# Linear attention and gated feed-forward: high weight words converted in PSUM, integer additions on GpSimd, k and v loaded as 112 and 3 rows, a new order

## The chip, the cores and the metric

The kernel runs on one core of a Trainium2 chip. The metric is the device time of one execution in microseconds. The kernel before was run three times: 1007.83, 1008.34 and 1012.99 us, median 1008.34. One execution was also profiled.

## The reference

Eight batches, eight heads, 576 tokens, head dimension 64; then a gated feed-forward network with 4608 tokens, model width 512 and inner width 1536.

```python
q_s = exp(q - max(q, -1)); q_s /= sum(q_s, -1) + 1e-9          # over the head dimension
k_s = exp(k - max(k, 2));  k_s /= sum(k_s, 2) + 1e-9           # over the tokens
kv  = einsum('bhsd,bhse->bhde', k_s, v)
x   = einsum('bhsd,bhde->bhse', q_s, kv)  ->  (4608, 512)
xn  = x / sqrt(mean(x * x, -1) + 1e-6) * rms_g
g   = xn @ w_gate
out = (g * sigmoid(g) * (xn @ w_val)) @ w_out
```

The three weight matrices arrive as float64, so each number is two 32-bit words, and the kernel makes float32 of them itself.

## The kernel before, in words

**Stages.** The 4608 tokens are cut into 9 blocks of 512. In each block the inner width is cut into 12 tiles of 128, so the feed-forward part has 108 steps, numbered `s` = 0 to 107. For one step, `f1` multiplies the block's x with a gate tile and a value tile (into two `ps_gv` banks of PSUM), `g_mul`, `silu` and `h_mul` combine them, and `f2` multiplies the result with a tile of the output weights and adds it up in four `ps_o` banks. Attention for the heads runs in pairs `g` = 0 to 3, per batch for k and v (`k_load`, `k_max`, `k_tr`, `k_top`, `k_diag`, `k_rows`, `k_sub`, `k_exp`, `k_mm`) and per block for q (`q_...`), and is spread between the feed-forward steps of the blocks before. Its PSUM tiles come from two `ps_a` banks, those of batch 0 from the `ps_o` banks, which are not yet in use then.

**Split products.** TensorE multiplies in a faster, shorter float32 format (float32r). A number is split into a high part (`w_hi`, `o_hi`, `h_hi`, a cast) and a low part (`w_lo`, `o_lo`, `h_lo`, number minus high part), and three products are added: `f1` is 24 matmuls in all, `f2` 12. For tiles 0 to 8 there is no `h_hi`, `h_lo`, `o_hi`, `o_lo`, and `f2` multiplies in plain float32, with four matmuls that the trace shows as two records each. Line 855 chooses the form. Copies and casts are recorded at line 329, products with a scalar at 334 (ScalarE) and 336 (VectorE).

**Weight conversion.** For tile `i` (0 to 11) and matrix `a` (gate, value, out), `load_w` (line 359) brings 512 columns of two-word numbers into a raw buffer. There are four raw buffers, two of which lie in the place of the later tiles' finished weights (line 319). `conv_low` (370, ScalarE) scales the low words to the three bits that belong to the fraction. `conv_mul` (374, ScalarE) scales the high words as floats, straight into the finished tile `W`. `conv_shift` (377) shifts that tile in place by three bits and clears the sign, `conv_sign` (382) puts the sign back from the raw word, both on VectorE. `conv_add` (387) adds the low bits as integers, on VectorE (letter D) or GpSimd (letter P, and without a letter). Gate and value are converted together (1024 columns) from tile 1 on, the output weights alone (512).

**Order.** All steps are written out in one string, `ORDER`, and issued in that order; each engine runs its own instructions strictly in it. A name is a step, its numbers are its arguments, and a letter says the engine: A ScalarE, D VectorE, P GpSimd. All DMAs are issued by SyncE, also in that order, so a load that waits for its buffer holds the loads behind it. `warm.n` are matmuls without use that keep TensorE busy.

**k and v loads.** From batch 1 on, 576 tokens lie as 115 rows of 5 tokens and one row with the last token. `k_load` (line 415) issues one DMA for the 115 rows of both heads (422) and one for the last row (423). `v_load` (438) issues one for the 115 rows of each head (446) and one for the last row (449). Batch 0 lies as 96 rows of 6.

Of the kernel before, what the change touches and what calls it, by code (L numbers as in the profile page):

```python
# [27 lines left out]
k_diag.0.1:A load_w.0.2 k_mm.0.0 q_exp.0.1 k_load.1.0 k_max0.0.2 k_rows.0.1 warm.2.2 q_eps0.0.0 k_max0.0.3 load_w.2.0
k_tr.0.2 warm.2.6 load_w.2.1 warm.2.10 load_w.1.2 q_rec0.0.0 k_top.0.2 k_tr.0.3 load_w.3.0 q_mul0.0.0:D k_diag.0.2:A
load_w.3.1 k_rows.0.2 k_sub.0.1 q_sub0.0.2:P warm.2.11 q_load0.1.0 q_max0.0.3 q_t0.0.0 k_exp.0.1 q_sum0.0.1  # L30
q_sub0.0.3:P q_exp.0.2 load_w.2.2 k_top.0.3 warm.2.3 q_c0.0.0:A k_sub.0.2 k_load.1.1 k_diag.0.3:A k_mm.0.1 q_exp.0.3
k_eps.0.0 q_eps0.0.1 load_w.3.2 k_rec.0.0 k_exp.0.2 q_rec0.0.1 q_sum0.0.2 k_rows.0.3 q_mul0.0.1:P warm.2.7
# [5 lines left out]
v_load.1.0 q_c0.0.3:A x_lo.0.1 q_x0.0.2 conv_mul.0.2.1:A conv_sign.0.1.1 n_sum0.1 conv_add.0.0.1:D conv_mul.1.0.2:A
x_hi.0.2:D conv_add.0.1.1:P q_x0.0.3 x_sq.0.2 k_max.1.0 conv_mul.2.0.2:A n_sum0.2 x_lo.0.2 x_sq.0.3 warm.2.8 warm.2.13
x_hi.0.3:A w_hi.0.0.2:D n_sum0.3 conv_low.2.0.2 conv_shift.1.0.2 x_lo.0.3 w_lo.0.0:P f1.0.0.0.0 f1.0.1.0.0  # L40
conv_mul.1.2.1:A f1.0.0.0.1 n_t.0 f1.0.0.0.2 conv_low.1.2.1 f1.0.0.0.3 f1.0.1.0.1 w_lo.0.1:D f1.0.1.0.2 f1.0.1.0.3
f1.0.0.1.0 n_y0.0 f1.0.0.1.1 conv_low.3.0.2 f1.0.0.1.2 conv_sign.1.0.2 f1.0.0.1.3 f1.0.1.1.0 f1.0.1.1.1 f1.0.1.1.2
f1.0.1.1.3 n_y1.0 conv_mul.3.0.2:A f1.0.0.2.0 conv_add.1.0.2:P f1.0.0.2.1 f1.0.0.2.2 f1.0.0.2.3 f1.0.1.2.0 f1.0.1.2.1
f1.0.1.2.2 conv_mul.2.2.1:A f1.0.1.2.3 q_max0.1.0 k_tr.1.0 conv_low.2.2.1 n_rows.0 q_sub0.1.0:P w_hi.1.0.2:A k_top.1.0
g_mul.0 v_ones.1.1 k_diag.1.0:A v_load.1.1 q_exp.1.0 w_lo.1.0:D k_rows.1.0 f1.1.0 silu.0 conv_shift.0.2.1 w_lo.1.1:D
conv_sign.0.2.1 conv_shift.2.0.2 conv_mul.3.2.1:A h_mul.0 conv_add.0.2.1:P conv_low.3.2.1 k_sub.1.0 f1.1.1 load_w.4.0
conv_sign.2.0.2 k_exp.1.0 load_w.4.1 load_w.4.2 q_sum0.1.0 conv_add.2.0.2:D f2.0 q_eps0.1.0 w_hi.2.0.2:D q_rec0.1.0
# [5 lines left out]
conv_low.5.0.2 load_w.6.1 w_lo.3.1:D load_w.6.2 f1.3.0 conv_shift.4.0.2 conv_mul.5.0.2:A q_max0.1.1 kv_lo.1.0:P
conv_low.5.2.1 conv_sign.4.0.2 conv_mul.5.2.1:A q_sub0.1.1:D f1.3.1 conv_add.4.0.2:D q_exp.1.1 g_mul.3 w_hi.4.0.2:D
silu.3 f2.2 q_sum0.1.1 w_lo.4.0:D conv_shift.3.2.1 conv_low.6.0.2 q_eps0.1.1 conv_sign.3.2.1 q_rec0.1.1 conv_low.6.2.1
h_mul.3 conv_add.3.2.1:P conv_mul.6.0.2:A k_max.1.2 k_tr.1.1 f1.4.0 q_mul0.1.1:P load_w.7.0 conv_mul.6.2.1:A
load_w.7.1 k_top.1.1 q_max0.1.2 k_diag.1.1:A load_w.7.2 q_load.2.0 w_lo.4.1:D conv_shift.5.0.2 k_rows.1.1 f1.4.1
# [5 lines left out]
conv_low.8.0.2 conv_sign.5.2.1 h_mul.5 w_lo.6.1:P conv_low.8.2.1 n_cols.0 v_ones.1.3 conv_add.5.2.1:D v_load.1.3
conv_shift.7.0.2 f1.6.0 q_eps0.1.2 conv_sign.7.0.2 q_rec0.1.2 conv_add.7.0.2:D f1.6.1 q_mul0.1.2:D w_hi.7.0.2:A
load_w.10.0 g_mul.6 load_w.10.1 load_w.10.2 w_lo.7.0:D silu.6 q_load.2.1 conv_shift.6.2.1 w_lo.7.1:D k_tr.1.2 f2.5
conv_sign.6.2.1 k_top.1.2 h_mul.6 conv_add.6.2.1:P k_diag.1.2:A k_max.1.3 conv_mul.8.0.2:A conv_shift.7.2.1 q_max0.1.3
conv_mul.8.2.1:A k_rows.1.2 q_t0.1.2 conv_shift.8.0.2 conv_low.10.0.2 f1.7.0 k_sub.1.2 q_sub0.1.3:P q_c0.1.2:A
# [859 lines left out]
```

## Time and profile before

| | |
|---|---|
| runs, us | 1007.83, 1008.34, 1012.99 |
| profiled execution, us | 1011.01 |
| its span, first to last instruction, us | 1009.2 |
| mean granted TensorE clock | 0.998 |
| TensorE busy | 992.5 us, 98% of the span, 4884 matmul records |
| VectorE busy | 514.4 us, 51% |
| ScalarE busy | 595.5 us, 59% |
| GpSimd busy | 683.5 us, 68% |
| read from and written to memory | 47.25 MB and 9.44 MB |

In the profile PE is TensorE, PEld its weight loads, DVE VectorE, ACT ScalarE, POOL GpSimd, SP SyncE (SPq its queue of DMA issues). `L826` is line 826 of the kernel. Times count from the first instruction. A line such as `ps_gv<-xh,wh` says what is written and what is read. Busy time is time in which at least one instruction of the engine runs, so the times of single instructions, which overlap a little, add up to slightly more.

### The profile page before, as it was taken

The numbers are of one execution on the slowest core, as the hardware profiler recorded it, in microseconds if no ns is written. First come the engines' busy times: TensorE is split into PE (matmuls) and PEld (weight loads), VectorE is DVE, ScalarE is ACT, GpSimd is POOL, SyncE is SP. The second block draws the span as 40 slices with busy tenths as digits, with TensorE's granted clock in tenths as the row PEclk, the third lists the DMA queues.
The fourth block names the chain that finished last, engine by engine and source line by source line (L and its number), as shares of the span: only waits on it lengthen the run. The fifth ranks groups of instructions, "written<-read, shape, count | busy, mean of one in ns | idle before, by whom it ended". The sixth has DMA issues, their size and how long they took to land.

```text
span 1009.2 us, 14153 instructions
## 1 busy us (share of the span) xinstructions
PE 992.5 (98%) x4884; PEld 795.7 (79%) x4884; DVE 514.4 (51%) x1191; ACT 595.5 (59%) x832; POOL 683.5 (68%) x601
## 2 busy tenths in 40 slices
...
DMA packets 128507, 57.60 MB, mean 57 GB/s; under 512 B 100620, under 2 KB 122420, under 8 KB 128436
## 3 DMA queue, kind: packets, MB, share of 16 engines
...
HBM read 47.25 MB, written 9.44 MB: 56 GB/s over the span
## 4 chain that ended last, share of the span: by engine, by line
PE 92%; SPq 4%; DMA 4%; ACT 0%; issue 0%; DVE 0%; ACTq 0%
PE ps_gv L826 57%; PE ps_o L865 29%; PE ps_a L704 2%; PE ps_a L505 2%; DMA w<-in_moe_w_out_dram 1%; SPq L365 1%; DMA w<-in_moe_w_val_dram 1%; SPq L446 1%; DMA raw<-in_moe_w_out_dram 1%; PE ps_a L487 1%; SPq L449 1%; DMA w<-in_k_dram 1%; SPq L443 0%; PE ps_a L754 0%; PE ps_a L633 0%; SPq L587 0%
## 5 line engine op out<-in xcount | busy, mean ns | idle before, releaser
L803 POOL TENSOR_TENSOR wl<-w,wh 128x512 fp32r<-128x512 f32 x203 | 262.2, 1300 | 107.3 <-ACT wh L329 81.3
L826 PE MATMUL ps_gv<-xh,wh 128*128 128x512 f32 x864 | 240.4, 400 | 0.9 <-ACT wh L329 0.7
L826 PE MATMUL ps_gv<-xl,wh 128*128 128x512 f32 x864 | 232.4, 391 | 0.0
L826 PE MATMUL ps_gv<-xh,wl 128*128 128x512 f32 x864 | 232.1, 391 | 0.0
L826 PEld LDWEIGHTS ps_gv<-xl,wh 128*128 128x128 f32 x864 | 162.8, 188 | 35.2
L826 PEld LDWEIGHTS ps_gv<-xh,wl 128*128 128x128 f32 x864 | 162.8, 188 | 35.0
L826 PEld LDWEIGHTS ps_gv<-xh,wh 128*128 128x128 f32 x864 | 157.1, 188 | 36.2 <-issue 1.9
L831 DVE TENSOR_TENSOR gs<-ps_gv,r 128x512 f32<-128x512 f32 x108 | 74.5, 690 | 214.9 <-PE ps_gv L826 189.1
L835 ACT ACTIVATE gs<-gs 128x512 f32<-128x512 f32 x108 | 68.3, 633 | 162.8 <-DVE gs L831 162.3
L847 POOL TENSOR_TENSOR hl<-gs,hh 128x512 fp32r<-128x512 f32 x99 | 129.0, 1303 | 14.9 <-ACT hh L329 14.4
L838 DVE TENSOR_TENSOR gs<-ps_gv,gs 128x512 f32<-128x512 f32 x108 | 74.2, 687 | 122.2 <-PE ps_gv L826 117.1
L811 POOL TENSOR_TENSOR ol<-w,oh 128x512 fp32r<-128x512 f32 x99 | 128.8, 1302 | 9.5 <-ACT oh L329 7.6
L329 ACT CAST wh<-w 128x1024 fp32r<-128x1024 f32 x92 | 96.6, 1050 | 40.6 <-PE ps_gv L826 31.9
L865 PE MATMUL ps_o<-oh,hh 128*128 128x512 f32 x396 | 108.8, 395 | 0.0
L865 PE MATMUL ps_o<-ol,hh 128*128 128x512 f32 x396 | 106.6, 390 | 0.0
L865 PE MATMUL ps_o<-oh,hl 128*128 128x512 f32 x396 | 106.6, 390 | 0.0
L329 ACT CAST oh<-w 128x512 fp32r<-128x512 f32 x99 | 61.3, 619 | 74.5 <-PE ps_o L865 73.9
L865 PEld LDWEIGHTS ps_o<-ol,hh 128*128 128x128 f32 x396 | 74.3, 188 | 16.0
L865 PEld LDWEIGHTS ps_o<-oh,hl 128*128 128x128 f32 x396 | 74.4, 188 | 15.9 <-POOL hl L847 0.2
L865 PEld LDWEIGHTS ps_o<-oh,hh 128*128 128x128 f32 x396 | 72.5, 188 | 14.3
L329 ACT CAST hh<-gs 128x512 fp32r<-128x512 f32 x98 | 60.7, 619 | 38.1 <-DVE gs L838 37.6
L835 ACT ACT_TABLE_LOAD x50 | 64.2, 1283 | 5.8 <-DVE gs L831 5.0
...
## 6 DMA issues: line engine op xcount, KB each, us to landing
...
```

Of the source, the lines that this page charges most:

```text
L329: (e.copy if e is nc.scalar else e.tensor_copy)(dst, src)
L365: nc.sync.dma_start(t.rearrange("p (c f) -> p c f", c=NKT), src)
L505: nc.tensor.matmul(ps[h * D:(h + 1) * D, :D + 1], lhsT=ke[:n, h, j], rhs=vt[:n, j, h], start=(j == 0), stop=(j == len(rows) - 1))
L704: nc.tensor.matmul(px[:, c0:c1], lhsT=wt, rhs=mv[:, c0:c1], start=(i == 0), stop=(i == 2))
L803: on(nc.gpsimd).tensor_tensor(out=wl[:, a], in0=W(s % NF, a), in1=wh[:, a].bitcast(F32), op=ALU.subtract)
L811: on(nc.vector).tensor_tensor(out=ol, in0=W(s % NF, 2), in1=wo_[s][0].bitcast(F32), op=ALU.subtract)
L826: nc.tensor.matmul(pd[s], lhsT=m[:, a, c * P:(c + 1) * P], rhs=X[j, c][x], start=(n == 1), stop=(n == 3 * NKT))
L831: nc.vector.tensor_tensor(out=gs, in0=g_[s], in1=r_[s // NF], op=ALU.mult)
L835: nc.scalar.activation(g_[s], g_[s], AF.Silu)
L838: nc.vector.tensor_tensor(out=g_[s], in0=v_[s], in1=g_[s], op=ALU.mult)
L847: on(nc.gpsimd).tensor_tensor(out=hl, in0=g_[s], in1=h_[s][0].bitcast(F32), op=ALU.subtract)
L865: nc.tensor.matmul(po[t], lhsT=a[:, t * P:(t + 1) * P], rhs=w, start=(i == 0 and n == 0), stop=(i == NF - 1 and n == len(terms) - 1))
```

## The change

- `conv_mul` writes 512 columns into a fresh tile of the two `ps_a` banks instead of into `W`. `conv_shift` works in place there. `conv_sign` reads that tile and the raw word and writes `W`. All three now take one matrix at a time: 36 of each instead of 25.
- All 25 `conv_add` run on GpSimd; before, ten of 1024 columns and two of 512 ran on VectorE.
- k and v of batches 1 to 7 are loaded as 112 rows, 3 rows and the last row: three issues instead of two for k, five instead of three for v.
- The first half of the order is new (up to step 99; the rest is the same text). With it engines change: `w_lo` has 1 instead of 13 on VectorE (215 instead of 203 on GpSimd), `w_hi` 5 instead of 16 on VectorE (103 instead of 92 on ScalarE), and of batch 0 and 1 some `q_sub0`, `q_mul0`, `q_c0`, `x_hi`, `kv_norm0` leave VectorE. `h_hi`, `h_lo`, `o_hi`, `o_lo` exist from tile 4 instead of 9, which gives `f2` of tiles 4 to 8 the split form. The useless matmuls are 37 instead of 44. In the new order `f1` of step 0 stands before three of the four `n_sum0`, pair 1 of batch 0 is worked on last, and `load_w` of tiles 4, 6, 9 and 10 stands before the `v_load` that it followed.

```diff
-    def conv_mul(i, a, n):
-        scaled(W(i, a, n), raw_words(i, a, n, 1).bitcast(F32), 2.0 ** -112, nc.scalar)
-
-    def conv_shift(i, a, n):
-        dst = W(i, a, n).bitcast(I32)
-        nc.vector.tensor_scalar(out=dst, in0=dst, scalar1=3, scalar2=0x7FFFFFFF,
+    cv = {}
+
+    def conv_mul(i, a):
+        cv[i, a] = ps_a.tile([P, TB], F32, name="ps_a")
+        nc.scalar.mul(cv[i, a], raw_words(i, a, 1, 1).bitcast(F32), 2.0 ** -112)
+
+    def conv_shift(i, a):
+        t = cv[i, a].bitcast(I32)
+        nc.vector.tensor_scalar(out=t, in0=t, scalar1=3, scalar2=0x7FFFFFFF,
                                 op0=ALU.logical_shift_left, op1=ALU.bitwise_and)
-    def conv_sign(i, a, n):
-        dst = W(i, a, n).bitcast(I32)
-        nc.vector.scalar_tensor_tensor(out=dst, in0=raw_words(i, a, n, 1), scalar=SIGN, in1=dst,
-                                       op0=ALU.bitwise_and, op1=ALU.bitwise_or)
+    def conv_sign(i, a):
+        nc.vector.scalar_tensor_tensor(out=W(i, a).bitcast(I32), in0=raw_words(i, a, 1, 1), scalar=SIGN,
+                                       in1=cv[i, a].bitcast(I32), op0=ALU.bitwise_and, op1=ALU.bitwise_or)
...
+    ROWS = (slice(0, FULL // 16 * 16), slice(FULL // 16 * 16, FULL))
...
-        nc.sync.dma_start(kt[:FULL], k[b, hs, :SF].rearrange("h (p j) d -> p h j d", j=CH))
+        for r in ROWS:
+            nc.sync.dma_start(kt[r], k[b, hs, CH * r.start:CH * r.stop].rearrange("h (p j) d -> p h j d", j=CH))
...
-        for h in range(2):
-            nc.sync.dma_start(
-                vt[:FULL, :, h, :D],
-                v[b, 2 * g + h, :SF].rearrange("(p j) d -> p j d", j=CH))
+        for r in ROWS:
+            for h in range(2):
+                nc.sync.dma_start(vt[r, :, h, :D],
+                                  v[b, 2 * g + h, CH * r.start:CH * r.stop].rearrange("(p j) d -> p j d", j=CH))
```

The new order around the first feed-forward steps, as an example of how densely the converted columns are placed:

```diff
+n_sum0.0 v_load.1.0 q_c0.0.3:A k_rec.0.1 conv_sign.0.1 conv_low.0.1.1 warm.2.6 q_x0.0.3 k_max.1.0 kv_norm0.0.1:A
+conv_add.0.1.1 conv_mul.1.0 q_x0.0.1 x_sq.0.3 conv_shift.1.0 w_hi.0.0.2:A warm.2.4 x_hi.0.1:D warm.2.8 conv_sign.1.0
+x_sq.0.1 warm.2.7 w_lo.0.0:P x_hi.0.3:A f1.0.0.0.0 x_lo.0.1 n_sum0.1 conv_mul.1.1 x_lo.0.3 w_lo.0.1:P f1.0.0.0.1
...
+f1.3.0 conv_sign.3.2 conv_low.6.0.2 conv_sign.4.2 conv_add.3.2.1 conv_mul.5.0 k_max.1.2 w_hi.4.0.2:A conv_add.4.2.1
+load_w.7.0 f2.2 conv_shift.5.0 conv_mul.5.1 load_w.7.1 g_mul.3 load_w.7.2 conv_low.6.2.1 w_lo.4.0:P load_w.8.0
+conv_shift.5.1 silu.3 load_w.8.1 conv_sign.5.0 load_w.8.2 w_lo.4.1:P conv_sign.5.1 conv_mul.5.2 q_sum0.1.2
+conv_add.5.0.2 k_tr.1.1 f1.4.0 o_hi.4:A k_top.1.1 h_mul.3 k_diag.1.1:A conv_shift.5.2 q_sum0.1.3 conv_low.7.0.2
```

## Rows read from the trace of the kernel before

**Rows 1.** Windows: stretch, length; busy PE, PEld, DVE, ACT, POOL; clock, DMA, GB/s.

```profile
0.00:35.70 35.70, 28.34 (x182) 17.54 (x183) 28.09 (x67) 20.80 (x36) 13.07 (x38) 1.00 1.06 261
35.70:80.60 44.90, 39.70 (x167) 26.79 (x166) 40.76 (x74) 31.34 (x40) 14.36 (x13) 1.00 0.71 211
80.60:109.30 28.70, 28.70 (x120) 19.24 (x120) 27.09 (x46) 16.93 (x24) 5.03 (x5) 0.94 0.56 155
109.30:193.80 84.50, 84.50 (x424) 64.80 (x422) 62.15 (x137) 61.59 (x89) 68.16 (x57) 1.00 0.29 80
193.80:1005.00 811.20, 811.20 (x4002) 667.32 (x3996) 355.83 (x868) 464.35 (x645) 582.85 (x490) 1.00 0.14 33
```

**Rows 2.** Chain of waits in order of time: start, length, what.

```profile
71.70 6.04 DMA w<-in_moe_w_out_dram
...
96.51 3.43 PE ps_o L865 x8
...
146.44 2.72 PE ps_o L865 x12
```

**Rows 3.** Timeline, 62 to 81 us: start, length, instruction, idle before.

```profile
62.48 5.76 SPq L446 DMA_DIRECT2D vt<-in_v_dram  x2
...
77.83 0.67 ACT L372 ACTIVATE w<-w 128x512 int32<-128x512 uint32 x1 [0.47 <-DMA w<-in_moe_w_out_dram]
...
80.41 0.48 PE L487 MATMUL ps_a<-cm,ones 128*116 128x128 f32 x2 [2.83 <-ACT cm L334]
```

**Rows 4.** Groups of VectorE, 20 to 140 us: busy us, mean ns, idle before.

```profile
L379 DVE TENSOR_SCALAR w<-w 128x1024 int32<-128x1024 int32 x11 | 8.8, 798 | 0.4 <-ACT w L334 0.3
L803 DVE TENSOR_TENSOR wl<-w,wh 128x512 fp32r<-128x512 f32 x13 | 8.7, 681 | 0.0
L384 DVE SCALAR_TENSOR_TENSOR w<-raw,w 128x1024 int32<-128x1024 int32 x6 | 7.3, 1219 | 0.0
...
L389 DVE CUSTOM_DVE_ANT_0 w<-w,w 128x2048 uint16<-128x2048 uint16 x5 | 6.4, 1274 | 0.0
...
L329 DVE CAST wh<-w 128x1024 fp32r<-128x1024 f32 x5 | 3.4, 684 | 0.0
```

**Rows 5.** Groups of instructions over the whole span, by form.

```profile
L329 ACT CAST wh<-w 128x1024 fp32r<-128x1024 f32 x92 | 96.6, 1050 | 40.6 <-PE ps_gv L826 31.9 <-DVE w L389 7.7 <-POOL w L389 0.4
...
L726 DVE SCALAR_TENSOR_TENSOR xl<-ps_a,g_sb,xh 128x512 fp32r<-128x512 f32 x32 | 23.6, 738 | 16.2 <-ACT sq L721 10.7 <-ACT acc L721 5.5
...
L721 ACT ACTIVATE sq<-ps_a 128x512 f32<-128x512 f32 x24 | 14.2, 593 | 7.4 <-PE ps_gv L826 4.3 <-DVE xl L726 3.1
...
L334 ACT ACTIVATE w<-raw 128x512 f32<-128x512 f32 x9 | 6.1, 674 | 0.0
...
L329 DVE COPY qT<-ps_o 128x512 f32<-128x512 f32 x2 | 1.4, 682 | 0.0
```

**Rows 6.** Groups of GpSimd instructions, 20 to 60 us.

```profile
L803 POOL TENSOR_TENSOR wl<-w,wh 128x512 fp32r<-128x512 f32 x2 | 3.3, 1666 | 5.9 <-DVE sm L609 3.9 <-DMA w<-in_moe_w_val_dram 2.0
L389 POOL TENSOR_TENSOR w<-w,raw 128x1024 int32<-128x1024 int32 x1 | 2.4, 2443 | 3.6 <-DVE ps_a L775 3.6
```

**Rows 7.** Groups of GpSimd instructions, 160 to 210 us.

```profile
L803 POOL TENSOR_TENSOR wl<-w,wh 128x512 fp32r<-128x512 f32 x11 | 14.1, 1294 | 1.5 <-ACT wh L329 1.5
```

**Rows 8.** Timeline at 34 us, VectorE and GpSimd.

```profile
34.04 0.69 DVE L379 TENSOR_SCALAR w<-w 128x1024 int32<-128x1024 int32 x1
34.21 1.65 POOL L803 TENSOR_TENSOR wl<-w,wh 128x512 fp32r<-128x512 f32 x1 [2.01 <-DMA w<-in_moe_w_val_dram]
```

**Rows 9.** Windows: the time in which one k load of 115 rows arrives.

```profile
198.30:201.50 3.20, 3.20 (x16) 2.65 (x15) 1.99 (x6) 3.17 (x5) 1.44 (x3) 1.00 0.29 95
```

**Rows 10.** Timeline at the start of f1, ScalarE and TensorE.

```profile
21.36 0.68 ACT L334 ACTIVATE w<-raw 128x512 f32<-128x512 f32 x1
...
35.16 1.13 PE L748 MATMUL ps_a<-sq,mean_w 128*128 128x512 f32 x2 [0.65 <-ACT sq L721]
35.72 0.79 PE L826 MATMUL ps_gv<-xh,wh 128*128 128x512 f32 x1
```

More of the change, by code (lines that the diff above doesn't have):

```diff
@@ L28 @@
[L28 to L32, printed above, removed]
@@ L38 @@
[L38 to L42, printed above, removed]
@@ L43 @@
[L43 to L47, printed above, removed]
@@ L53 @@
[L53 to L57, printed above, removed]
@@ L63 @@
[L63 to L67, printed above, removed]
@@ new lines @@
+w_hi.33.0.2:A q_max.4.3 h_hi.31:A w_lo.33.0:P q_half.4.3 h_lo.31:P f1.32.0 o_hi.32:A w_lo.33.1:P o_lo.32:P k_tr.3.3
+f1.32.1 g_mul.32 k_top.3.3 silu.32 q_max2.4.3 q_sub.4.3:P k_diag.3.3:A q_exp.4.3 k_rows.3.3 h_mul.32 f2.31 k_sub.3.3
+h_hi.32:A q_sum.4.3 k_exp.3.3 h_lo.32:P q_half2.4.3 w_hi.34.0.2:A k_mm.3.3 q_sum2.4.3 q_rec.4.3 o_hi.33:A f1.33.0
+w_lo.34.0:P k_load.4.1 k_eps.3.3 k_rec.3.3 kv_hi.3.3:A w_lo.34.1:P kv_lo.3.3 o_lo.33:P q_x.3.3 g_mul.33 silu.33
+f1.33.1 k_max.4.1 v_ones.4.1 q_mul.4.3:P v_load.4.1 q_t.4.1 x_hi.3.3:A x_sq.3.3 x_lo.3.3 f2.32 q_load.5.0
@@ new lines @@
+q_mul.6.0:P n_sum.4 h_mul.47 w_hi.49.0.2:A f2.46 n_t.4 h_hi.47:A w_lo.49.0:P n_y0.4 q_hi.5.0:A q_hi.5.1:A n_y1.4
+q_lo.5.0:P f1.48.0 o_hi.48:A h_lo.47:P n_rows.4 n_cols.4 w_lo.49.1:P k_tr.5.0 f1.48.1 g_mul.48 o_lo.48:P k_top.5.0
+silu.48 k_diag.5.0:A q_lo.5.1:P k_rows.5.0 h_mul.48 w_hi.50.0.2:A f2.47 k_sub.5.0 h_hi.48:A w_lo.50.0:P k_exp.5.0
+h_lo.48:P f1.49.0 store.3.0:A w_lo.50.1:P store.3.1:A o_hi.49:A o_lo.49:P k_mm.5.0 g_mul.49 f1.49.1 k_eps.5.0
+k_load.5.2 silu.49 k_rec.5.0 kv_hi.5.0:D kv_lo.5.0 store.3.2:A q_x.5.0 h_mul.49 w_hi.51.0.2:A f1.50.0 q_t.5.2
```

446 lines of the change are left out of this document (229 added, 217 removed).

## The prediction, made before the changed kernel was run

> **What bounds the kernel now.** I read the windows first, then the chain of waits, then the issues behind its one late knot, and last the groups of the two engines that the change shifts work between.
>
> The windows [rows 1] cut the run at the first feed-forward matmul (35.7 us), at the end of TensorE's last wait (80.6 us) and at the start of `f1.16.0` (193.8 us). From 80.6 to 1005 us TensorE is busy in every microsecond: what follows 80.6 us only gets shorter if it has less to multiply, or nothing if a new wait appears. Before that, from 35.7 to 80.6 us, it works 39.70 of 44.9 us: 5.2 us of waits. VectorE is then busy for 40.76 of the 44.9 us and ScalarE for 31.34; GpSimd has 14.36 and 5.03 us of work in 44.9 and 28.7 us. So the first 110 us are VectorE's, with GpSimd nearly empty. The change moves work from the one to the other.
>
> The chain of waits [rows 2] runs through DMA until an output-weight load that lands at 77.7 us, and after that through TensorE alone: eight matmul records of `f2` in 3.43 us where its operands are plain float32, twelve in 2.72 us where they are split.
>
> The issues behind that load [rows 3]: SyncE is held for 5.76 us by the first two issues of one v load before it reaches the weights of tile 6. ScalarE, in order, converts them at 77.83 us with `k_diag.1.1` queued behind, and the matmul that needs it starts at 80.41 us, after 2.83 us of waiting. The granted clock of the next 28.7 us is 0.94 [rows 1], so part of it ran at 1.2 instead of 2.4 GHz: 0.06 x 28.7 = 1.7 us. This one knot costs 4.5 us.
>
> **Part 1: five split tiles more.** `h_hi`, `h_lo`, `o_hi`, `o_lo` exist from tile 4 instead of 9, so `f2` of tiles 4 to 8 changes form: 5 x (3.43 - 2.72) = **-3.6 us**, all on TensorE's unbroken chain [rows 2]. The splits put ten instructions each on ScalarE and on GpSimd; they are in the balances below. This gain is the surest term.
>
> **Part 2: VectorE.** It loses ten 1024-column additions at 1.274 (12.7 us), twelve `w_lo` at 0.681 (8.2) and eleven `w_hi` casts at 0.684 (7.5) [rows 4]: 28.4 us. Shift and sign go from 11 pairs and 14 single columns to 36 single columns. Before: shift 11 x 0.798, and half of that for the 14 singles, 14.4 us; sign 11 x 1.219 plus 14 x 0.61, 22.0 us. A shift from PSUM to PSUM and a sign from SBUF and PSUM to SBUF don't occur in this trace. The nearest rows are a copy out of PSUM at 0.682 and a three-operand instruction on PSUM at 0.738 [rows 5]; below them stand the old in-place prices, 0.40 and 0.61. I take 0.70 for both, near the copy: 36 x 1.40 = 50.4, or 14.0 more than the old 36.4 (0 more at the low end, 16.7 at 0.738). Net VectorE is **14 us lighter** (12 to 28), of the 96 us that it works before 109.3 us [rows 1]. That ends no chain by itself; it takes VectorE away as a cause of TensorE's waits before 80.6 us.
>
> **Part 3: ScalarE.** The multiplication into PSUM is bounded by the same one into SBUF, 0.674, and by a read of PSUM at 0.593 [rows 5]. I take 0.65: 36 x 0.65 = 23.4 against at most 36 x 0.674 = 24.3 before: nothing. Eleven `w_hi` casts at 1.050 [rows 5] and ten splits of half that size come, 17 us, spread over the stretch up to `f1.16.0`; after 80.6 us ScalarE has 79 us of work in 113 [rows 1]. Covered; if not, `w_hi` is late and TensorE waits at the next `f1`.
>
> **Part 4: GpSimd.** Between the first `f1` and `f1.16.0` its list grows from 68 to 104 instructions: ten 1024-column additions at 2.443 [rows 6], and 26 others (11 `w_lo`, 5 `o_lo`, 5 `h_lo`, five single ones) at 1.294 to 1.666 [rows 6, 7]. At the lower price that is 24.4 + 33.6 = 58 us on top of 14.36 + 5.03 + 68.16 = 87.6 [rows 1], 145.6 us, in a stretch of 158.1 us that should shrink to about 150: 97% full. VectorE, the fullest engine of before, reached 27.09 of 28.7 us, 94%, with TensorE never idle [rows 1]. So GpSimd is just past what has been seen to cost nothing: 145.6 / 0.94 = 155 us if that were a ceiling, 5 us above 150; nothing if it can be packed tighter. I take a little under half, **+2 us** (0 to +5).
>
> The price of one instruction decides here, and rows differ: 1.666 for `w_lo` between 20 and 60 us [rows 6], 1.294 between 160 and 210 [rows 7]. The slow one at 34.21 us ran beside an in-SBUF shift of VectorE [rows 8], the kind that the change takes away. The Trainium skill, "VectorE: DVE Perf Modes", section "Why PSUM operands drop a tier", says that an operand in PSUM keeps a float32 instruction out of the mode that uses both SBUF read ports, and "GPSIMD Engine Reference", section "1. Specifications", names that mode, and two SBUF inputs, as what contends with GpSimd. By that rule the shift loses its fast mode, which the range of part 2 holds, and GpSimd's price stays at the low end; part 4 would then cost 0 to +2 and the sum be about 1 us lower.
>
> **Part 5: k and v as 112 and 3 rows, and SyncE's order.** While one k load of 115 rows was all that moved, DMA ran at 0.29 of the 16 engines [rows 9], some 4.6 of them, and the load took 3.2 us. If 112 rows use more of them, it lands up to 2 us earlier; if not, nothing changes. Each k load has one issue more and each v load two, 84 in all; most come after 193.8 us, where DMA is busy for 0.14 of the time [rows 1] and loads have room. If they had not, k would be late and its pair's `k_tr` would hold TensorE. In the new order tiles 4, 6, 9 and 10 are loaded ahead of the v load that preceded them, so the 5.76 us [rows 3] no longer stand before tile 6. The order puts `k_diag.1.1` behind tile 6's first conversions still, but with tile 6 issued about a tile earlier. I take the knot as gone: **-4.5 us** (0 if ScalarE meets another late load there). The other 2.4 us of waits before 80 us I leave.
>
> The Trainium skill, "DMA: Bandwidth & Descriptors", section "Why a DMA increments its semaphore by 16 and not by 1", says a transfer is split over the largest number up to 16 that divides its row count. That is 5 engines for 115 rows and 16 for 112, agrees with the 4.6, and would make the load about 1 us.
>
> **Part 6: the start.** `f1` began at 35.72 us [rows 10], behind four statistics matmuls (`n_sum0`, about 1.1 us each, the last in rows 10), three of which the new order puts after its first chunk; that is no gain by itself. It now waits for `w_hi.0`, on ScalarE. The first conversion began at 21.36 [rows 10]; from it to the end of `w_hi.0` the new order gives ScalarE 17 instructions, at about 0.65 [rows 5] 11 us, so 32 to 33 us, and the displaced statistics (3.3 us) follow. Equal: **0** (-2 to +2). Seven fewer warm-up matmuls lie in waiting time.
>
> **Sum:** -3.6 + 2 - 4.5 + 0 = -6.1 us. The profiled execution took 1011.0 us (span 1009.2), 2.7 above the median of 1008.34; against itself it becomes 1004.9, and the median **1002.2 us**.
>
> **Rivals.**
> - *All of it comes back.* With VectorE light, every wait before 80.6 us goes and `f1` starts 2 us earlier: -3.6 - 5.2 - 1.7 - 2 = -12.5, **995.8**. For it: VectorE's 91% there. Against: GpSimd's 97%. Chance 0.20.
> - *The two PSUM banks.* The 36 converted columns now pass through the two banks of `ps_a`, which batch 1 also needs for 16 tiles (transpose, k product, q transpose, q product of four pairs). TensorE, in order, waits for a bank until VectorE has shifted and signed it: if half of the 16 wait one such pair, 8 x 1.4 = 11.2 us, against the 10.5 of part 1 and all the waits and the low clock of before, so **1009**, no change. For it: at nine of the 16 the order has the other bank still in use. Against: VectorE, lighter, clears a bank sooner. Chance 0.20.
> - *GpSimd becomes the bound (slower).* If half of the 56 `w_lo`, `o_lo`, `h_lo` of the stretch take 1.666 instead of 1.294, it has 145.6 + 28 x 0.37 = 156 us and, at 94%, the stretch takes 166 instead of 158.1, the gain of part 1 within it: **1016**. It decides from 149 us of work (158.1 x 0.94), that is, from nine such slow instructions on. Chance 0.15.
> - *112 rows do nothing*, and the late load stays on the chain: -3.6 + 2 = **1006.7**. Chance 0.05.
>
> **How the numbers follow.** The forecast has 0.40, with its own range 998 to 1006. About 0.5% (5 us) is what a measurement of this kernel can tell from no change: below 1003.3 is faster, above 1013.4 slower. Faster: 0.20 + 0.33 of the forecast's share + 0.02 = 0.55. Same: the banks' 0.20, 0.07 of the forecast and 0.03 = 0.30. Slower: 0.15. The range for 8 in 10 runs from 994.5, just past the first rival, to 1010, past the banks; GpSimd's rival is left out.
>
> **What would show it.** In the changed profile: `f2` of tiles 4 to 8 in twelve records of 2.72 us in all; VectorE's share of the first 110 us near 80%; GpSimd near 95% between the first `f1` and `f1.16.0` with single instructions near 1.29; k loads landing in about 1 us; TensorE unbroken from about 80 us and `f1.16.0` near 187.7. Wrong would be TensorE waits after 90 us on `wl` (GpSimd) or, in `ps_a` instructions, on VectorE's sign; a first `f1` later than 36 us; shift or sign above 0.8 us.

## The result, and the profile after

The changed kernel takes 1000.25 us (median of 6 runs, 999.24 to 1003.44), the kernel before, run beside it, 1010.75 (6 runs, 1007.83 to 1014.57): a ratio of 0.9902, interval 0.9877 to 0.9926. The profiled execution took 1000.02 us with a span of 998.2, which is 11.0 less than the 1009.2 of before. Forecast were 1002.2, and 6.1 us less. One profiled execution among those below, of the run with splits and additions on GpSimd, ran at a granted clock of 0.557 throughout and took 1653.57 us; its time and its trace are left out.

The windows of the changed kernel, cut as in [rows 1] (the last one ends at 990 us):

```profile
0.00:35.70 35.70, 31.07 (x182) 20.18 (x183) 27.32 (x61) 24.36 (x44) 19.43 (x45) 0.90 1.03 277
35.70:80.60 44.90, 42.68 (x180) 29.23 (x179) 40.40 (x80) 40.37 (x57) 37.21 (x28) 1.00 0.89 259
80.60:109.30 28.70, 28.70 (x144) 22.73 (x143) 24.69 (x43) 22.94 (x39) 27.41 (x20) 1.00 0.38 104
109.30:193.80 84.50, 84.50 (x448) 68.78 (x447) 59.83 (x152) 66.57 (x95) 80.91 (x70) 1.00 0.29 72
193.80:990.00 796.20, 796.20 (x3931) 655.15 (x3930) 332.10 (x834) 446.47 (x623) 568.83 (x479) 1.00 0.13 33
```

In the second window TensorE now waits 2.2 us instead of 5.2, and in the third the clock is 1.00 instead of 0.94. GpSimd has 37.21 + 27.41 + 80.91 = 145.5 us of work from 35.7 to 193.8 us, and from 80.6 us on it is 96% full without one TensorE wait. These windows no longer cut the same work as before: the first `f1` starts at 31.25 us and `f1.16.0` at 182.67, where 187.7 was forecast, and between the two GpSimd works 138.6 of 151.4 us, 92%. The clock of the first window, ahead of the first `f1`, is 0.90 here and 1.00 before; in the profiles below it lies between 0.90 and 1.00 with either order.

TensorE's timeline of the changed kernel (start, length, instruction, idle before; L495 is now `k_rows`, L481 `k_tr`, L628 `q_t0`, L390 `conv_sign`, L386 `conv_shift`, L376 `conv_low`):

```profile
31.25 0.39 PE L834 MATMUL ps_gv<-xh,wh 128*128 128x512 f32 x1
...
39.59 0.26 PE L481 MATMUL ps_a<-ident,cm 116*128 116x116 f32 x1
40.78 0.48 PE L495 MATMUL ps_a<-cm,ones 128*116 128x128 f32 x2 [0.94 <-ACT cm L338]
...
55.09 0.66 PE L628 MATMUL ps_a<-ident,xl 128*128 128x128 f32 x4 [0.74 <-ACT ot L338]
...
72.35 0.29 PE L481 MATMUL ps_a<-ident,cm 116*128 116x116 f32 x1 [0.55 <-DVE w L390]
75.26 0.38 PE L495 MATMUL ps_a<-cm,ones 128*116 128x128 f32 x2
...
88.58 1.07 PE L873 MATMUL ps_o<-oh,hh 128*128 128x512 f32 x4
...
91.30 1.14 PE L641 MATMUL ps_a<-qT,ot 128*128 128x64 f32 x4
```

From the first `f1` on, the three waits are all that is left. The `k_rows` that waited 2.83 us in [rows 3] starts at 75.26 without a wait. `f2` of tile 4 runs from 88.58 to 91.30, 2.72 us.

The groups of VectorE and GpSimd from 20 to 194 us (busy us and mean ns behind the bar), to set against [rows 4, 6, 7]:

```profile
L386 DVE TENSOR_SCALAR ps_a<-ps_a 128x512 int32<-128x512 int32 x36 | 24.4, 692 | 3.7 <-ACT ps_a L382 3.5
L390 DVE SCALAR_TENSOR_TENSOR w<-raw,ps_a 128x512 int32<-128x512 int32 x21 | 14.0, 679 | 0.1
...
L390 DVE SCALAR_TENSOR_TENSOR w<-w,ps_a 128x512 int32<-128x512 int32 x15 | 9.9, 679 | 0.1
...
L811 POOL TENSOR_TENSOR wl<-w,wh 128x512 fp32r<-128x512 f32 x36 | 47.1, 1322 | 4.0 <-ACT wh L333 2.8 <-DMA qt<-in_q_dram 1.2
```

Shift and sign in PSUM cost 0.692 and 0.679 us (taken: 0.70). GpSimd's `w_lo` lies at 1.322, near the low end of [rows 6, 7].

### The profile page after: what moved, and what is told of

It reads as the page before. It is cut to its first block, busy times and chain, and to the rows that moved or that the text cites. A ratio compares the mean times of both kernels' runs of the same rounds, so it can differ in the third digit from the quotient of the medians.

```text
span 998.2 us, 14424 instructions
## 1 busy us (share of the span) xinstructions
PE 987.5 (99%) x4897; PEld 799.2 (80%) x4897; DVE 485.6 (49%) x1170; ACT 602.9 (60%) x857; POOL 735.1 (74%) x640
## 4 chain that ended last, share of the span: by engine, by line
PE 92%; DMA 4%; SPq 2%; ACT 0%; POOL 0%; issue 0%; DVE 0%; POOLq 0%; ACTq 0%; DVEq 0%
PE ps_gv L834 58%; PE ps_o L873 29%; PE ps_a L712 2%; PE ps_a L513 2%; DMA w<-in_moe_w_val_dram 2%; DMA kt<-in_k_dram 1%; DMA vt<-in_v_dram 1%; PE ps_a L495 1%; SPq L451 1%; DMA raw<-in_moe_w_val_dram 1%; SPq L455 0%; SPq L369 0%; PE ps_a L762 0%; PE ps_a L641 0%; PE ps_a L481 0%
## 5 line engine op out<-in xcount | busy, mean ns | idle before, releaser
L811 POOL TENSOR_TENSOR wl<-w,wh 128x512 fp32r<-128x512 f32 x215 | 278.3, 1300 | 113.9 <-ACT wh L333 100.3
L855 POOL TENSOR_TENSOR hl<-gs,hh 128x512 fp32r<-128x512 f32 x104 | 134.5, 1293 | 28.8 <-ACT hh L333 28.3
L819 POOL TENSOR_TENSOR ol<-w,oh 128x512 fp32r<-128x512 f32 x104 | 134.8, 1296 | 16.3 <-ACT oh L333 16.3
L333 ACT CAST wh<-w 128x1024 fp32r<-128x1024 f32 x103 | 107.9, 1049 | 48.6 <-PE ps_gv L834 44.7
L873 PE MATMUL ps_o<-oh,hh 128*128 128x512 f32 x416 | 114.6, 396 | 0.0
L873 PE MATMUL ps_o<-ol,hh 128*128 128x512 f32 x416 | 112.0, 390 | 0.0
L873 PE MATMUL ps_o<-oh,hl 128*128 128x512 f32 x416 | 111.9, 390 | 0.0
L873 PEld LDWEIGHTS ps_o<-ol,hh 128*128 128x128 f32 x416 | 78.1, 188 | 16.8
L873 PEld LDWEIGHTS ps_o<-oh,hl 128*128 128x128 f32 x416 | 78.1, 188 | 16.7 <-POOL hl L855 0.2
L873 PEld LDWEIGHTS ps_o<-oh,hh 128*128 128x128 f32 x416 | 76.3, 188 | 15.3 <-issue 0.4
```

Of the source, the lines that this page charges most:

```text
L333: (e.copy if e is nc.scalar else e.tensor_copy)(dst, src)
L811: on(nc.gpsimd).tensor_tensor(out=wl[:, a], in0=W(s % NF, a), in1=wh[:, a].bitcast(F32), op=ALU.subtract)
L819: on(nc.vector).tensor_tensor(out=ol, in0=W(s % NF, 2), in1=wo_[s][0].bitcast(F32), op=ALU.subtract)
L855: on(nc.gpsimd).tensor_tensor(out=hl, in0=g_[s], in1=h_[s][0].bitcast(F32), op=ALU.subtract)
L873: nc.tensor.matmul(po[t], lhsT=a[:, t * P:(t + 1) * P], rhs=w, start=(i == 0 and n == 0), stop=(i == NF - 1 and n == len(terms) - 1))
```

## The experiments

Each was timed against the kernel before on its own chip; the ratio is to that. The first four ask what each part does, taken back or done alone.

**k and v back in 115 rows, in the changed kernel.**

```diff
-    ROWS = (slice(0, FULL // 16 * 16), slice(FULL // 16 * 16, FULL))
+    ROWS = (slice(0, FULL),)
```

> The changed kernel with the k and v loads of batches 1 and later back in one piece of 115 rows. Theory (the loads have room, and what removed the late knot is the order in which SyncE issues): a k load alone takes 3.2 us again instead of about 1, the weights of tile 6 are still issued before 60 us, TensorE's first f1 and its last wait stay where they are, and the time is within 1.5 us of the changed kernel's 1000.3 (span 998 to 999.7). Rival (112 rows are what made the loads land in time): k_max.1.1 or the kernel-weight conversions meet a late load, TensorE waits 2.8 us or more before 90 us, and the time rises by 2.8 to 4.5 us, to 1003 to 1005.

Measured: 1008.35 us, 0.9976 (0.9962 to 0.9991), 8 us above the changed kernel. My theory fell, and the rival was still too small. Timeline of this run:

```profile
65.43 8.25 SPq L455 DMA_DIRECT2D vt<-in_v_dram  x2
73.73 1.72 SPq L457 DMA_DIRECT2D vt<-in_v_dram  x1
...
73.04 1.12 ACT L376 ACTIVATE w<-w 128x1024 int32<-128x1024 uint32 x1 [4.53 <-DMA w<-in_moe_w_val_dram]
...
78.22 0.29 PE L481 MATMUL ps_a<-ident,cm 116*128 116x116 f32 x1 [4.24 <-DVE w L390]
```

And SyncE at the same load in the changed kernel:

```profile
60.72 4.99 SPq L455 DMA_DIRECT2D vt<-in_v_dram  x4
65.75 0.61 SPq L457 DMA_DIRECT2D vt<-in_v_dram  x1
```

Five issues hold SyncE for 5.6 us where three held it for 10.0. But the weights for which ScalarE waits at 73.04 us, those of tile 6, were issued ahead of that load. In this run:

```profile
50.31 4.87 SPq L455 DMA_DIRECT2D vt<-in_v_dram  x2
...
62.46 0.55 SPq L369 DMA_DIRECT2D w<-in_moe_w_val_dram  x1
```

and in the changed kernel:

```profile
47.84 2.93 SPq L455 DMA_DIRECT2D vt<-in_v_dram  x4
...
58.75 0.51 SPq L369 DMA_DIRECT2D w<-in_moe_w_val_dram  x1
...
67.10 1.15 ACT L376 ACTIVATE w<-w 128x1024 int32<-128x1024 uint32 x1 [1.69 <-DMA w<-in_moe_w_val_dram]
```

Of the 5.9 us by which ScalarE gets these weights later (73.04 instead of 67.10), 3.7 are a later issue (2.5 of them already there at the v load shown) and 2.2 a longer way from issue to landing (10.6 instead of 8.4 us). The shift behind it is late, and `k_tr.1.1` waits 4.24 us for the PSUM bank. The hold of 10.0 us delays tile 7, for which ScalarE waits 0.64 us and TensorE not at all. So the largest wait comes from weights that are issued and land later, not from k or v. The waits at `k_rows` and `q_t0` grow by 1.0 us each (1.92 and 1.75); the second one the changed kernel has in some runs by itself (the repeated run below). What the rows of k and those of v do singly was not run.

**`f2` of tiles 4 to 8 plain again, in the changed kernel.** Twenty steps go out of the order, for i = 4 to 8:

```diff
-o_hi.i:A
-o_lo.i:P
-h_hi.i:A
-h_lo.i:P
```

> The changed kernel without h_hi, h_lo, o_hi, o_lo of tiles 4 to 8: their f2 is plain float32 again. Theory (TensorE's unbroken chain is what these five shorten, and GpSimd, though 96% full, delays nobody): f2 of tiles 4 to 8 has eight records of 3.43 us instead of twelve of 2.72, and the time rises by 3.6 us to 1003.9 (span 1001.8). Rival (GpSimd is the bound of the stretch to f1.16.0): with ten instructions, 13 us, less on GpSimd and ten less on ScalarE, the lows come earlier and TensorE's instructions close up; the time rises by less than 1.5 us, or falls.

Measured: 1005.59 us, 0.9949 (0.9930 to 0.9968), some 5 us above the changed kernel. In its timeline `f2` of tile 4 is one row again, and the next instruction starts 3.43 us after it:

```profile
90.81 3.59 PE L871 MATMUL ps_o<-w,gs 128*128 128x512 f32 x8
94.24 1.14 PE L639 MATMUL ps_a<-qT,ot 128*128 128x64 f32 x4
```

So 5 x 0.71 = 3.6 us is the price on TensorE, as forecast, and taking 13 us of work from GpSimd brought nothing back. The rest is a wait at `q_t0`, 2.27 us instead of 0.74, and a clock of 0.96 from 35.7 to 80.6 us, ahead of anything that this edit touches (see the repeated run below).

**The splits alone, in the kernel before.** Put into its order for i = 4 to 8, behind the later of `h_mul.i` and the tile's last addition:

```diff
+o_hi.i:A h_hi.i:A o_lo.i:P h_lo.i:P
```

> The kernel before, with h_hi, o_hi (ScalarE) and h_lo, o_lo (GpSimd) of tiles 4 to 8 put in, and nothing else. Theory (the split is worth its five f2 on TensorE's chain wherever GpSimd has room, and GpSimd of before has): 3.6 us less than before, 1007.1 against 1010.75 (span 1005.6). Rival (the splits' twenty instructions delay ScalarE's conversions and VectorE-made lows of the next tiles): TensorE waits on wh or wl between 80 and 120 us, and less than 1.5 us is left of the gain, or it is slower.

Measured: 1022.61 us, 1.0118 (1.0097 to 1.0140): 12 us slower. Its windows from 80.6 us:

```profile
80.60:109.30 28.70, 24.68 (x118) 17.96 (x116) 28.63 (x42) 16.36 (x24) 13.36 (x9) 0.99 0.51 144
109.30:193.80 84.50, 77.36 (x373) 62.43 (x374) 60.39 (x118) 59.09 (x87) 67.37 (x55) 0.92 0.28 78
```

TensorE, never idle there in [rows 1], waits 4.0 + 7.1 us and loses 0.08 x 84.5 = 6.8 us to the lower level of its clock. VectorE is full, 28.63 of 28.7, but that alone is not the cause: with the rows alone, below, it is just as full there (28.63) and TensorE never waits. What differs is the price of its instructions beside the added `o_lo` and `h_lo` on GpSimd:

```profile
101.38 2.20 DVE L391 CUSTOM_DVE_ANT_0 w<-w,w 128x2048 uint16<-128x2048 uint16 x1
103.50 1.76 DVE L615 TENSOR_TENSOR xl<-qt,sm 128x512 f32<-128x512 f32 x1
...
100.21 2.28 POOL L813 TENSOR_TENSOR ol<-w,oh 128x512 fp32r<-128x512 f32 x1 [4.31 <-ACT oh L331]
102.46 2.26 POOL L849 TENSOR_TENSOR hl<-gs,hh 128x512 fp32r<-128x512 f32 x1
```

In the kernel before the same two instructions of VectorE, an addition at 101.84 us and a product at 102.98, took 1.23 and 0.68 with GpSimd idle. From 80 to 194 us a sign of 1024 columns takes 1.50 to 1.72 us on average instead of 1.22 (with the rows alone 1.21 to 1.22), and `w_hi` on ScalarE waits 3.01 us for the addition shown. So the term that the prediction called surest did not hold where VectorE's instructions stretch beside GpSimd's. The places chosen here for the twenty steps are the only ones that were tried, and their share in the 12 us is open.

**The late load of tile 6, in the kernel before.** One step moved:

```diff
-v_load.1.2 kv_hi.1.0:A
+kv_hi.1.0:A
...
-load_w.6.2
+load_w.6.2 v_load.1.2
```

> The kernel before, with the one v load that held SyncE for 5.76 us moved behind the three weight loads of tile 6, and nothing else. Theory (the late load of tile 6 is the knot): tile 6 is issued by about 66 us, ScalarE does not wait at 77 us, the matmul of 80.41 us starts without its wait of 2.83 us, the clock does not fall behind it, and the time falls by 4.5 us (2.8 of wait, 1.7 of clock) to 1006.2 (span 1004.7). Rival 1 (only the wait goes, the clock falls for another wait): 2 to 3 us less. Rival 2 (ScalarE or VectorE meets the next late thing, tile 7 or the v of the second pair, so that the wait moves): within 1 us of before, with a TensorE wait of 2 us or more somewhere between 75 and 95 us.

Measured: 1009.38 us, 0.9978 (0.9965 to 0.9991): rival 2, nearly. The timeline shows a wait ahead of the first `f1`, which the moved step comes after and which is 1.1 us longer than in [rows 10], and the knot:

```profile
36.97 1.12 PE L748 MATMUL ps_a<-sq,mean_w 128*128 128x512 f32 x2 [1.76 <-ACT sq L721]
...
80.79 0.48 PE L487 MATMUL ps_a<-cm,ones 128*116 128x128 f32 x2 [1.90 <-ACT cm L334]
```

Tile 6 is issued at 63.45 us instead of 70.51, yet 1.90 of the 2.83 us stay, since ScalarE now comes late from tile 5, for which it waits 3.25 us up to 70.06. The clock behind the wait is 1.00. Moving one load doesn't untie the knot.

**112 and 3 rows alone, in the kernel before.** The change's edit of `k_load` and `v_load`, and nothing else of it:

```diff
+    ROWS = (slice(0, FULL // 16 * 16), slice(FULL // 16 * 16, FULL))
...
-        nc.sync.dma_start(kt[:FULL], k[b, hs, :SF].rearrange("h (p j) d -> p h j d", j=CH))
+        for r in ROWS:
+            nc.sync.dma_start(kt[r], k[b, hs, CH * r.start:CH * r.stop].rearrange("h (p j) d -> p h j d", j=CH))
```

> The kernel before, with nothing changed but the k and v loads in 112 and 3 rows. Theory from the run with 115 rows put back (115-row loads hold SyncE, and what is behind them lands late): the v load that held SyncE for 5.76 us before tile 6 holds it for under 4, tiles 5 and 6 are issued 2 us or more earlier against the first f1, the wait of 2.83 us at 80 us shrinks to under 1 and the clock behind it stays at 1.00, and the time falls by 3 to 5 us, to 1006 to 1008. Rival (before's order puts the v load ahead of tile 6 and keeps VectorE at 91%, so the rows pay only together with the new order): within 1.5 us of before.

Measured: 1004.65 us, 0.9945 (0.9928 to 0.9962): 5.5 us faster, the theory. The timeline at the place of [rows 3], where the kernel before issues tile 6 so:

```profile
70.51 0.54 SPq L365 DMA_DIRECT2D w<-in_moe_w_gate_dram  x1
```

and this run:

```profile
58.34 3.02 SPq L449 DMA_DIRECT2D vt<-in_v_dram  x4
61.41 0.61 SPq L451 DMA_DIRECT2D vt<-in_v_dram  x1
62.06 0.40 SPq L365 DMA_DIRECT2D w<-in_moe_w_gate_dram  x1
...
75.89 0.38 PE L489 MATMUL ps_a<-cm,ones 128*116 128x128 f32 x2
```

SyncE is held for 3.6 us instead of 5.76 + 2.17, and reaches this load 4.1 us earlier already (58.34 instead of 62.48); tile 6 is issued at 62.06 instead of 70.51, in the old order; the `k_rows` of the knot doesn't wait, and the clock is 1.00 up to 193.8 us. This one small part, alone, gives half of the change's gain.

**The ten large additions back on VectorE, in the changed kernel.** For i = 2 to 11:

```diff
-conv_add.i.0.2
+conv_add.i.0.2:D
```

> The changed kernel with its ten 1024-column additions of tiles 2 to 11 back on VectorE, in the new order. Theory (the additions had to leave VectorE for the splits to pay): VectorE, 97% full again between the first f1 and 110 us, is late with shift, sign and g_mul; TensorE waits on VectorE or on wh for 4 us or more after 36 us, and the time rises by 4 to 10 us, to 1004 to 1010. Rival 1 (GpSimd, 96% full, is what is near the edge): 24 us less of GpSimd let the lows come earlier, and the time is within 1 us of the changed kernel's or below it.

Measured: 1002.84 us, 0.9929 (0.9912 to 0.9946), 2 to 3 us above the changed kernel: between the two. TensorE waits 2.79 us at `q_t0` and 0.41 us on sign at 106 us, VectorE reaches 27.63 of 28.7 us. Taking 24 us from GpSimd brings nothing back. VectorE has the work instead, so this run alone doesn't say that the 96% cost nothing; the first profile does, where TensorE never waits after 80.6 us.

**The high words in SBUF, in the changed kernel.** Order and single columns stay.

```diff
-        cv[i, a] = ps_a.tile([P, TB], F32, name="ps_a")
+        cv[i, a] = W(i, a)
```

> The changed kernel with the scaled high words kept in the weights' own SBUF tile instead of a PSUM bank (the multiplication writes there, shift and sign work there in place), in the same order and the same single columns. Theory (PSUM is dearer for VectorE itself, and what it buys is GpSimd's price): shift 0.40 and sign 0.61 instead of 0.69 and 0.68, 13 us less on VectorE; GpSimd's w_lo before 80 us at 1.5 to 1.67 instead of 1.32, and its 1024-column additions above 2.5; GpSimd at 96% then makes TensorE wait on wl, and the time rises by 2 to 6 us. Rival (the banks were the cost): GpSimd's prices stay within 3%, the wait of 0.55 us on the bank at 72 us goes, and the time falls by 0.5 to 3 us.

Measured: 1020.89 us, 1.0106 (1.0089 to 1.0123): 20 us above the changed kernel, and not as I had said it. The groups of VectorE, 20 to 194 us:

```profile
L386 DVE TENSOR_SCALAR w<-w 128x512 int32<-128x512 int32 x36 | 40.4, 1138 | 2.7 <-ACT w L382 2.7
L390 DVE SCALAR_TENSOR_TENSOR w<-raw,w 128x512 int32<-128x512 int32 x21 | 22.2, 1069 | 0.1
L390 DVE SCALAR_TENSOR_TENSOR w<-w,w 128x512 int32<-128x512 int32 x15 | 16.1, 1087 | 0.1
```

In SBUF shift and sign are dearer, not cheaper: 40.4 + 22.2 + 16.1 = 78.7 us instead of the 24.4 + 14.0 + 9.9 = 48.3 that the same 36 pairs take in PSUM. The timeline of VectorE and GpSimd shows why:

```profile
112.23 2.27 DVE L386 TENSOR_SCALAR w<-w 128x512 int32<-128x512 int32 x1
114.53 1.66 DVE L390 SCALAR_TENSOR_TENSOR w<-raw,w 128x512 int32<-128x512 int32 x1
...
119.19 0.41 DVE L386 TENSOR_SCALAR w<-w 128x512 int32<-128x512 int32 x1
...
120.32 0.67 DVE L390 SCALAR_TENSOR_TENSOR w<-w,w 128x512 int32<-128x512 int32 x1
...
111.78 2.44 POOL L395 TENSOR_TENSOR w<-w,raw 128x1024 int32<-128x1024 int32 x1 [1.56 <-DVE w L390]
114.17 1.48 POOL L819 TENSOR_TENSOR ol<-w,oh 128x512 fp32r<-128x512 f32 x1
```

The shift that begins at 112.23 ends at 114.50, 0.28 us behind GpSimd's addition (114.22); the sign behind it ends at 116.19, 0.54 behind GpSimd's next instruction (115.65). From 119 to 121 us GpSimd runs nothing, and the same two take 0.41 and 0.67. `k_rows` in that place waits 5.51 us, TensorE's longest wait in this run. GpSimd pays less: `w_lo` 1.392 instead of 1.322 on average. The Trainium skill, "SBUF — State Buffer", section "SBUF: two separate sides", calls the pair of ports that VectorE and GpSimd share an exclusive lock, which goes for a whole instruction to whichever started first. These lines agree.

**Splits, and the additions on GpSimd, in the kernel before.** The order of the run with the splits alone and, for i = 2 to 11:

```diff
-conv_add.i.0.2:D
+conv_add.i.0.2:P
```

> The kernel before with the splits of tiles 4 to 8, as in the run that was 12 us slower, and with the ten 1024-column additions of tiles 2 to 11 on GpSimd instead of VectorE, nothing else. Theory (that run was slow because VectorE, at 28.63 of 28.7 us, came late with what TensorE needed next): VectorE falls under 90% from 80 to 110 us, TensorE's waits after 80 us shrink from 14 us to under 4, the clock stays at 1.00, and the time falls to 1005 to 1010. Rival (the twenty instructions of the split were put in at bad places, or GpSimd is late with its 2.44 us additions): TensorE still waits 8 us or more after 80 us, and the time stays above 1016.

Measured: 1027.45 us (four runs), 1.0172 (1.0153 to 1.0191): 17 us slower; the theory fell, and the rival's time held. There is no trace to read, so the rival's wait isn't shown; why the additions make it worse is for the run with all three parts.

**The changed kernel once more**, without an edit.

> The changed kernel itself once more, for its runs beside those of the other two here and as a measure for the runs with one part taken back, whose traces showed a wait of 2.3 to 2.8 us at q_t0 (55 us) and a granted clock of 0.96 up to 80 us where the changed kernel's first trace showed 0.74 us and 1.00, though none of them alters anything before that wait that could make it. Theory (that wait is the landing time of tile 5's weights, which differs from run to run): its runs fall into two groups some 3 us apart (1000 and 1003), and its ratio stays within 0.9877 to 0.9926. Rival (the wait is those edits' own doing): all its runs within 1 us of 1000.

Measured: 1001.17 us in 4 runs (999.17 to 1002.95), 0.9895 (0.9871 to 0.9919). The profiled execution was one of the longer ones, span 1001.2 instead of 998.2, and its timeline shows where the 3 us are:

```profile
47.53 0.40 SPq L369 DMA_DIRECT2D raw<-in_moe_w_gate_dram  x1
...
56.33 0.66 PE L628 MATMUL ps_a<-ident,xl 128*128 128x128 f32 x4 [2.55 <-ACT ot L338]
```

Tile 4 was issued 1.2 us later than in the first trace (46.30), ScalarE waited 3.6 us for it instead of 1.7, TensorE 2.55 at `q_t0`, and the clock from 35.7 to 80.6 us is 0.96. The wait that the experiments showed here is the changed kernel's own, not theirs. It is tile 4's weights that are late, not tile 5's, as I had written; the runs lie between 999 and 1003 rather than in two groups.

**Tile 4's weights before the first v load, in the changed kernel.** One step moved:

```diff
-n_sum0.0 v_load.1.0
+n_sum0.0
...
-load_w.4.2
+load_w.4.2 v_load.1.0
```

> The changed kernel with one step moved: the v load of batch 1's first pair goes behind the three weight loads of tile 4, which it now precedes by 5 us of issues. Theory (what is left of TensorE's waits is ScalarE waiting for weights that land late behind v loads): tile 4 is issued from 41.5 to 43 us instead of 46.3 to 47.8, ScalarE's two waits of 0.54 and 1.14 us for it go, TensorE's wait at q_t0 falls from 0.74 (2.3 to 2.8 in other runs) to under 0.3, the clock stays at 1.00, and the time falls by 0.7 us in the best case and by about 2 in the median, to 998 to 999.5. Rival (the v load is then late for its product): k_mm.1.0, at 50.11 us, waits for v by 1 us or more, TensorE with it, and the time is the same or up to 3 us longer.

Measured: 1002.99 us, 0.9923 (0.9902 to 0.9945): the rival. The late piece is now v:

```profile
53.58 1.44 PE L513 MATMUL ps_a<-vt,kt 116*64 116x65 f32 x20 [4.05 <-DMA vt<-in_v_dram]
```

**Rows, splits and additions together, in the kernel before.** Old order, words in SBUF: the edits of the two runs above, splits with additions on GpSimd and 112 and 3 rows alone, in one kernel.

> The kernel before with three of the change's parts together: k and v in 112 and 3 rows, the splits of tiles 4 to 8, and the ten 1024-column additions on GpSimd; its old order, and the high words in SBUF as before. Theory (what the words in a PSUM bank buy is that VectorE's shift and sign no longer stretch while GpSimd works): shift and sign of 1024 columns take 20% or more above the 0.80 and 1.22 us of before, single ones up to 2 us where they meet a GpSimd addition; VectorE is over 95% full from 80 to 194 us though 12.7 us were taken off it, TensorE waits 8 us or more in there on VectorE or on what follows it, and the time is 1015 to 1024. Rival 1 (the 12 and 18 us that the splits cost without the rows were late loads): 1000 to 1006. Rival 2 (GpSimd is late with its additions): GpSimd over 95% full from 80 to 194 us and TensorE's waits ending on wl, ol or hl.

Measured: 1025.08 us, 1.0138 (1.0118 to 1.0159), and no theory holds whole. Its windows from 80.6 us:

```profile
80.60:109.30 28.70, 22.57 (x105) 15.84 (x103) 22.83 (x35) 14.45 (x23) 18.20 (x11) 0.99 0.54 154
109.30:193.80 84.50, 74.46 (x357) 59.96 (x358) 56.74 (x110) 56.92 (x83) 73.41 (x57) 0.90 0.25 71
```

Shift of 1024 columns takes 0.928 on average (0.798 in [rows 4]), the single signs 1.03 to 1.10 us, so the stretching is there; but VectorE works only 22.83 of 28.7 us and GpSimd 18.20. Nobody is full. TensorE waits 16 us and loses 8.5 us to the clock (0.90 of 84.5) while the engines wait for each other: ScalarE's `w_hi` and `o_hi` 25.2 us in all for GpSimd's additions, which take 2.4 to 2.8 us where VectorE's took 1.27, and the old order puts the cast 2 to 6 steps behind them (the new one 6 to 16). So the additions on GpSimd seem to need the new order as well as the PSUM bank. The bank is shown by the run with the words in SBUF; the order is argued, as no run has the old order with the words in PSUM.

**Tile 4's weights before a q load, in the changed kernel.** One step moved:

```diff
-q_load0.1.2 conv_sign.0.0
+conv_sign.0.0
...
-load_w.4.2
+load_w.4.2 q_load0.1.2
```

> The changed kernel with one step moved: the q load of tile 1's third pair (four issues) goes from before batch 1's first v load to behind the three weight loads of tile 4. In the two traces of the changed kernel, tile 4 was issued at 46.30 and 47.53 us, ScalarE waited 1.7 and 3.6 us for it, and TensorE 0.74 and 2.55 us at q_t0, the second time with a granted clock of 0.96 up to 80 us. The v load itself can't go behind tile 4 (k_mm.1.0 then waited 4.05 us for it). Theory (the landing of tile 4 is what parts the two groups of runs): tile 4 is issued 2 us or more earlier, v stays in time, ScalarE's waits for tile 4 fall under 1 us, TensorE's at q_t0 under 0.3, the clock stays at 1.00 in every run, and all runs lie near or below the faster group, 998.5 to 1000, 1 to 2 us under the changed kernel's median. Rival (SyncE and the 16 DMA engines are full here, so that one load's gain is another's loss): q_max0.1.2, at 56.35 us on VectorE, waits for the q load by 1 us or more and with it shift and sign of tile 4; the time is 1000 to 1004.

Measured: 1000.59 us (999.64 to 1004.60), 0.9902 (0.9885 to 0.9919): the changed kernel's ratio. In the profiled execution (span 997.8) tile 4 is issued at 43.80 us and `q_t0` doesn't wait, as the theory says; but one run of six is still 4 us longer, and what remains to be had is below what the runs can tell apart. No version beat the changed kernel.

## Why the prediction was right, and where it was not

Right were the sign and the place (everything before 80.6 us, and five `f2`). The size was not: -6.1 was forecast, and -11.0 measured in spans (-10.5 in medians). That the time came within 2 us of 1002.2 is luck, since the kernel before took 1010.75 beside it, 2.4 us more than the 1008.34 from which the forecast counted. GpSimd's load looks right to 0.1 us (145.5 for 145.6) only in windows that no longer cut the same work; in the stretch that was meant it is 138.6 us. Point by point, in spans:

- **Part 1, -3.6.** Measured 5 x (3.43 - 2.72) = 3.6. "The surest term" was wrong as a judgement: the splits alone cost 12 us.
- **Part 2, shift and sign in PSUM.** The price was right (0.69 and 0.68 for 0.70 taken). The comparison was not: it set them against 0.40 and 0.61, halves of 1024-column prices from a kernel whose GpSimd was nearly empty there; the single ones of before took 0.494 and 0.69 on average, so that the old sum was 38.7 rather than 36.4. Beside a full one, SBUF costs 1.14 and 1.08, so the bank saves VectorE 30 us where the prediction charged it 14 more. It had the reason in hand, in part 4, but applied it to GpSimd's price only.
- **Part 3, nothing.** Holds: no TensorE wait ends on `wh`.
- **Part 4, +2.** Measured 0: no wait on `wl`, `ol` or `hl` at 96%, and a GpSimd relieved by 13 us gave nothing back. VectorE's 94% without a wait was no ceiling for another engine.
- **Part 5, -4.5.** The knot is gone in full (2.83 of wait, 1.7 of clock), but the step that removed it was misnamed. It credited the order; one move of that order alone gave 1.6, the rows alone 5.5, and the whole change without the rows 2.6 (1008.35 against 1010.99). It asked of the rows only how early k lands ("up to 2 us earlier", from [rows 9]) and counted their issues; that [rows 3] show two issues of 115 rows holding SyncE, and that fewer busy engines might be why, it did not put together. The link between the two is still argued: the runs show that the rows shorten the hold, not how. As for the landing, a window of the changed kernel as a k load of 112 rows comes in:

```profile
187.50:188.50 1.00, 1.00 (x6) 0.82 (x5) 0.94 (x5) 0.00 (x0) 0.63 (x1) 1.00 0.83 220
```

  DMA runs at 0.83 instead of 0.29 and moves 220 GB/s instead of 95. That agrees with the Trainium skill, "DMA: Bandwidth & Descriptors", section "Why a DMA increments its semaphore by 16 and not by 1", by which 112 rows go to 16 engines and 115 to 5, though the 280 KB take somewhat more than the 1 us that was worked out from it.
- **Part 6, 0.** Measured -2.0: `f1` of step 0 starts at 31.25 instead of 35.72 and, with the three statistics matmuls inside it, ends where `k_tr.1.0` starts, at 39.59 instead of 41.61 in the kernel before:

```profile
41.61 0.26 PE L473 MATMUL ps_a<-ident,cm 116*128 116x116 f32 x1
```

  It comes with the order: in every profile of the new order the first `f1` starts between 30.38 and 31.46 us, whatever part was taken out, and in every one of the old between 34.77 and 37.53.
- **Left out.** The pair of warm-up matmuls that the old order had at tile 19 stood in the unbroken chain: about 0.5 us.

The other waits stay at 2.2 us. -3.6 - 4.5 - 2.0 - 0.5 = -10.6. The last `f2` record starts 10.7 us earlier than before (993.94 instead of 1004.63); the other 0.3 of the 11.0 lie behind it.

Of the rivals, *all of it comes back* (-12.5) came nearer than the forecast: of its terms the five `f2`, the knot's wait, the clock and the 2 us of the start all came, and only 2.2 us of waits stayed. Its reason, a light VectorE, is not what did it: with the rows alone the knot and the low clock went with VectorE as full as before. The banks' was real in kind and small: one wait of 0.55 us on sign. It grows to 4.24 when weights come late. GpSimd never became the bound, since its `w_lo` stayed at 1.32; with the words in SBUF it is 1.39, so what the PSUM bank keeps cheap is VectorE, far more than GpSimd.
